# Two levels of Strassen's method for the first product of a fused attention and feed-forward kernel

The kernel runs on one core of one Trainium2 chip. The metric is the device time of one execution in microseconds (us), the median of several. Engines are named as the profile names them: PE is TensorE's matmul, PEld its weight load, DVE VectorE, ACT ScalarE, POOL GpSimd, SP SyncE, which issues most transfers.

## The reference

```python
# q, k, v: (8, 8, 576, 64) f32; w_in: (512, 2048); w_out: (2048, 512)
kv  = einsum('bhsd,bhse->bhde', k, v)
out = einsum('bhsd,bhde->bhse', q, kv)
x   = out / sqrt(mean(out*out, -1) + 1e-6) * g_norm      # per head
x   = x.transpose(0, 2, 1, 3).reshape(4608, 512)
h   = x @ w_in
g   = maximum(0.01 * h, h)
return g @ w_out
```

## The kernel before

The 4608 rows are worked off in nine blocks of 512. Block 0 uses plain matmuls. From block 1 on, each block is four chunks of 512 hidden columns, and both products of a chunk (h, the first; o, the second) use one level of Strassen's method in Winograd's form: seven products of quarters instead of eight, each four fp32 matmuls with 256 moving columns. The h product of a chunk is interleaved with the o product of the chunk before, and the attention of the next batch is fed in between, one step at every odd slot of the 28 slots (4 chunks x 7 products) of a block.

```python
ORDER = (1, 2, 6, 5, 7, 3, 4)
def strassen(which, left, right, done):
    for i in ORDER:
        ...                                   # two PSUM banks, "a" and "c"; 1, 2, 5 start one
        for part in range(2):
            for r in range(2):
                matmul(bank[:, part, :], lhsT=left(i, part, r), rhs=right(i, part, r), ...)
        done(i, bank)                         # eviction: ACT copy or DVE add into SBUF
        yield
# in product_h, done():  g21, g22, ... = bank sums; relu on ACT;
#   s1..s4 = sums of g on GpSimd, the left sides of the o product
...
for i in range(1, NB):                        # blocks
    a_steps = attention(i + 1) if i + 1 < B else iter(())
    for c in range(NC):                       # chunks
        h_steps = product_h(h_sides, x_sides, g_sides)
        for t in range(7):
            go(h_steps, 1)
            go(o_steps, 1)
            ...                               # sides of w_in and w_out on GpSimd
            if (7 * c + t) % 2:
                go(a_steps, 1)
            if c == NC - 1 and t == 4 and i + 1 < NB:
                go(a_steps)
                x_sides, more_x = sides_x(xTs.pop(i + 1))   # sides of x on VectorE
        o_steps = product_o(c, o_next, g_sides, os, store(i))
```

## Time and profile before

| | before |
|---|---|
| median (lowest to highest) | 978.23 us (977.07 to 978.3) |
| PE busy, share of the span | 954.6 us, 98% |
| DVE / ACT / POOL busy | 430 / 270 / 508 us |
| bytes moved by DMA | 63.5 MB |

### The profile page before, as it was taken

Reading aid. Unit: us, or ns where it says so; the run is one execution under the profiler, and the core shown is the slowest. Engines: PE = TensorE matmul, PEld = TensorE weight load, DVE = VectorE, ACT = ScalarE, POOL = GpSimd, SP = SyncE. Lnnn points to the kernel's source line nnn. Section 1 sums busy time; section 2 is a strip of 40 time slices with the busy share of each in tenths; the row PEclk is TensorE's granted clock in tenths of the full one; section 3 lists DMA queues with packets and bytes.
Section 4 is the critical chain, followed back from the end, with each engine's and each line's share of the span. In section 5 each row is a group of like instructions: output and inputs, shape, how many; then the busy total and the mean of one; then the engine's idle time right before and its main releaser. Section 6 shows DMA issues by size and latency. Waiting matters only on the chain.

```text
span 974.5 us, 14053 instructions
## 1 busy us (share of the span) xinstructions
PE 954.6 (98%) x5702; PEld 762.3 (78%) x5702; DVE 430.2 (44%) x688; ACT 270.1 (28%) x531; POOL 507.9 (52%) x399
## 2 busy tenths in 40 slices
PE   8899998999999999999999999999999999999997
PEld 4444345888888888888888888888888888888886
DVE  3966873256224543256224832373235422431223
ACT  3634531232123311332123212331223121112210
POOL 1000203556655565666665665566565766666664
PEclk9899998999999999999999999999999999999999
DMA  9989702500152004300430044002200000001001
GB/s 248 215 217 252 197 1 84 153 1 1 40 149 50 1 11 130 97 1 1 141 97 1 1 126 111 1 1 65 77 1 1 11 33 1 1 12 33 1 0 44
DMA packets 36161, 63.48 MB, mean 65 GB/s; under 512 B 4864, under 2 KB 21248, under 8 KB 36096
## 3 DMA queue, kind: packets, MB, share of 16 engines
q1 hardware_dynamic: 26112, 51.95, 20.8%
q10 hardware_dynamic: 9856, 10.62, 3.2%
q8 instruction: 45, 0.74, 0.3%
q14 instruction: 20, 0.16, 0.1%
q0 software_dynamic: 128, 0.00, 0.0%
HBM read 53.12 MB, written 9.44 MB: 64 GB/s over the span
## 4 chain that ended last, share of the span: by engine, by line
PE 94%; DVE 2%; DMA 2%; ACT 1%; issue 0%; SPq 0%; ACTq 0%
PE h_a L87 23%; PE o_a L87 23%; PE h_c L87 17%; PE o_c L87 17%; PE h_ps L87 5%; PE o_acc L87 5%; PE o_ps L87 2%; DMA k_in<-in_k_dram 2%; PE kv_ps L87 2%; DMA raw<-in_moe_w_in_dram 1%; DVE w L199 0%; DVE w L201 0%; ACT cut L194 0%; DVE qT L329 0%; DVE xT L309 0%
## 5 line engine op out<-in xcount | busy, mean ns | idle before, releaser
L405 POOL TENSOR_TENSOR ws<-w 128x512 f32<-128x512 f32 x33 | 46.4, 1407 | 288.6 <-PE h_c L87 247.7
L405 DVE TENSOR_TENSOR o<-o_a,o 128x512 f32<-128x512 f32 x104 | 71.6, 688 | 203.3 <-PE o_a L87 203.2
L484 ACT ACTIVATE g<-g 128x512 f32<-128x512 f32 x96 | 60.5, 630 | 292.5 <-DVE g L405 292.5
L405 POOL TENSOR_TENSOR ws<-w,w 128x512 f32<-128x512 f32 x33 | 43.5, 1318 | 150.5 <-ACT cut L194 101.4
L87 PE MATMUL o_a<-wt,gs 128*128 128x256 f32 x512 | 120.9, 379 | 0.0
L87 PEld LDWEIGHTS o_a<-wt,gs 128*128 128x128 f32 x512 | 97.3, 190 | 13.2
L405 DVE TENSOR_TENSOR o<-o_c,o 128x512 f32<-128x512 f32 x88 | 60.5, 687 | 89.5 <-PE o_c L87 89.5
L405 POOL TENSOR_TENSOR wt<-w,wt 128x512 f32<-128x512 f32 x64 | 83.2, 1300 | 2.5
L405 POOL TENSOR_TENSOR gs<-g,g 128x512 f32<-128x512 f32 x64 | 83.2, 1323 | 0.3 <-ACT g L484 0.2
L405 DVE TENSOR_TENSOR g<-h_c,g 128x512 f32<-128x512 f32 x64 | 44.0, 688 | 85.6 <-PE h_c L87 85.6
L87 PE MATMUL h_ps<-xT,w 128*128 128x512 f32 (+1 forms) x136 | 60.2, 588 | 6.9 <-DVE xT L309 6.1
L87 PE MATMUL o_acc<-w,gT 128*128 128x512 f32 x128 | 60.7, 619 | 3.7 <-DVE w L201 3.7
L87 PE MATMUL h_a<-xT,w 128*128 128x256 f32 x256 | 61.2, 382 | 0.7 <-ACT g L484 0.7
L87 PE MATMUL o_a<-w,g 128*128 128x256 f32 x256 | 60.6, 379 | 0.8 <-DVE o L405 0.8
L87 PE MATMUL h_a<-xt,w 128*128 128x256 f32 x256 | 61.1, 382 | 0.0
L87 PE MATMUL h_c<-xT,w 128*128 128x256 f32 x256 | 61.1, 381 | 0.0
L87 PE MATMUL h_a<-xt,ws 128*128 128x256 f32 x256 | 61.1, 381 | 0.0
L87 PE MATMUL h_a<-xT,ws 128*128 128x256 f32 x256 | 61.1, 381 | 0.0
L87 PE MATMUL h_c<-xt,ws 128*128 128x256 f32 x256 | 61.1, 381 | 0.0
L87 PE MATMUL o_c<-wt,gs 128*128 128x256 f32 x256 | 60.5, 379 | 0.0
L87 PE MATMUL h_c<-xT,ws 128*128 128x256 f32 x256 | 60.5, 379 | 0.0
L87 PE MATMUL o_a<-wt,g 128*128 128x256 f32 x256 | 60.5, 379 | 0.0
(84 smaller groups left out, 1607.6 us busy)
## 6 DMA issues: line engine op xcount, KB each, us to landing
out_dram<-o ACTq DMA_DIRECT2D x36, 256.0 KB, 2.2
v_in<-in_v_dram SPq DMA_DIRECT2D x30, 288.0 KB, 4.9
raw<-in_moe_w_in_dram SPq DMA_DIRECT2D x64, 128.0 KB, 5.8
raw<-in_moe_w_out_dram SPq DMA_DIRECT2D x16, 512.0 KB, 6.8
k_in<-in_k_dram SPq DMA_DIRECT2D x28, 288.0 KB, 4.2
q_in<-in_q_dram SPq DMA_DIRECT2D x56, 144.0 KB, 4.5
q_in<-in_q_dram SPq DMA_DIRECT2D x56, 140.0 KB, 4.5
k_in<-in_k_dram ACTq DMA_DIRECT2D x2, 288.0 KB, 9.2
```

The lines of the kernel that those rows point to most:

```text
L87: pin(nc.tensor.matmul(*args, **kw))
L405: eng.tensor_tensor(out_, a, b_, op=ALU.subtract if minus else ALU.add)
L484: nc.scalar.activation(t, t if src is None else src, func=AF.Prelu, alpha=SLOPE)
```

## The change

The intent is to take columns off PE. From block 2 on the h product uses two levels: each of the seven products of quarters is itself done by seven products of smaller blocks, 49 matmuls of 128 x 128 x 128 instead of 28 with 256 columns. They run in two groups: products 1, 6, 7, 4 of the outer level together (banks h_ha and h_hc, four parts each), then 2, 5, 3 (h_hb and h_ob, three parts). The 49 combinations of w_in are made once, in block 1, written to DRAM, and read again per block into a ring of nine places. The sides of x get a second level too (`quarters`). The cut diff:

```diff
+    def combine(c):                       # block 1: quarters of w_in, to DRAM
+        for js, y in (((5, 6), pair(0, ...)), ((7, 3), pair(1, ...)), ((1, 2), direct), ((4,), last)):
+            add(nc.vector, s1, y21, y22)
+            add(nc.vector, s2, s1, y11, True)
+            add(nc.vector, s3, y11, y21, True)
+            add(nc.vector, s4, y12, s2, True)
+            ...                           # three dma_start per j on SyncE
+    reads = [(c, j) for _ in range(2, NB) for c in range(NC) for j in ALL]
+        def quarters(group):              # second level of the sides of x
+            for js, y in of[group]:
+                add(nc.vector, t[:, :, 0, :], y12, y11, True)
+                add(nc.vector, t[:, :, 1, :], y22, t[:, :, 0, :], True)
+                add(nc.vector, y12, y22, y12, True)
+                add(nc.vector, t[:, :, 2, :], y21, t[:, :, 1, :], True)
+    def product_h_two(i, c, to):
+        for group, tags, out_ in ((0, ("ha", "hc"), g), (1, ("hb", "ob"), qc)):
+            for k in ORDER:
+                for n, j in enumerate(js):
+                    matmul(banks[b][:, n, :], lhsT=w_place(base + n)[:, SLOT[k], :],
+                           rhs=x_sides[j][k], ...)
+                ...                       # eviction: ACT copy or DVE add
+                if group == 0 and k == 4:
+                    for n in range(1, 4): # three running sums
+                        add(nc.gpsimd, g[:, :, n, :], g[:, :, n, :], g[:, :, n - 1, :])
+                    relu(g[:, :, 3, :])
+                yield
+            read(base + len(js) + RING)
+        add(nc.vector, g[:, :, 0, :], g[:, :, 0, :], qc[:, :, 0, :])   # merges of the groups
+        ...                               # three more, relus on ACT
+        sums()                            # s1..s4 on GpSimd, as before
     for i in range(1, NB):
+        if i > 1:
+            quarters(1)
         for c in range(NC):
             for t in range(7):
-                go(h_steps, 1)
+                go(h_steps, 1 if one else 2)
                 go(o_steps, 1)
                 if (7 * c + t) % 2:
                     go(a_steps, 1)
+                if c == NC - 1 and i + 1 < NB:
+                    if t == 3:
+                        go(a_steps)
+                        x_sides, first, second, quarters = sides_x(i + 1)
+                        first()
+                    if t == 4 and not one:
+                        second()
+                        quarters(0)
```

More of the change, by code (lines that the diff above doesn't have):

```diff
@@ L73 @@
     consts = ctx.enter_context(tc.tile_pool(name="consts", bufs=1))
-    stage = ctx.enter_context(tc.tile_pool(name="stage", bufs=3))
+    dram = ctx.enter_context(tc.tile_pool(name="dram", bufs=1, space=bass.MemoryType.DRAM))
     ins = ctx.enter_context(tc.tile_pool(name="ins", bufs=2))
@@ L77 @@
     xpool = ctx.enter_context(tc.tile_pool(name="xpool", bufs=3))
-    wcomb = ctx.enter_context(tc.tile_pool(name="wcomb", bufs=1))
     gpool = ctx.enter_context(tc.tile_pool(name="gpool", bufs=2))
@@ L84, with view, pair @@
     pin = tc.keep_in_program_order
+    NW = U * NE * P
+    w1_all = consts.tile([P, 2 * NC * NW], F32, name="w1_all")
+    stage = consts.tile([P, 3 * NW], F32, name="stage")
+    pairs = consts.tile([P, 4 * NW], F32, name="pairs")
+    g_all = [consts.tile([P, 4 * U * N2], F32, name=f"g_{i}") for i in range(2)]
+    def view(t, lo, *shape):
+        n = 1
+        for d in shape:
+            n *= d
+        t = t[:, lo:lo + n]
+        names = "abcd"[:len(shape)]
+        return t.rearrange(f"p ({' '.join(names)}) -> p {' '.join(names)}",
+                           **dict(zip(names, shape))) if len(shape) > 1 else t
+    def pair(i, *shape):
+        return view(pairs, i * NW, *shape)
     def matmul(*args, **kw):
@@ L129, in load_first @@
         qs += [rows(early[:, i * n:]) for i in range(2)]
-        ks, vs = (t + [rows(wcomb.tile([P, 4 * U * P], F32, tag=f"pair{i + j}",
-                                       name="early_kv")) for i in range(2)]
-                  for j, t in ((0, ks), (2, vs)))
+        ks, vs = (t + [pair(i + j, J, D) for i in range(2)] for j, t in ((0, ks), (2, vs)))
         for way, to, src, ts, p in (
@@ L141 @@
     kvs = [consts.tile([P, NP, D], F32, name=f"kv_{i}") for i in range(2)]
-    zeros = gpool.tile([P, NT], F32, tag="g11", name="zeros")
+    zeros = view(g_all[0], 0, NT)
     nc.gpsimd.memset(zeros, 0.0)
     load_first()
-    w1_sb = [[consts.tile([P, U, NE, P], F32, name=f"w1_{h}_{c}") for c in range(NC)]
-             for h in range(2)]
+    w1_sb = [[view(w1_all, (2 * c + h) * NW, U, NE, P) for c in range(NC)] for h in range(2)]
     w2_sb = [[consts.tile([P, U, DM], F32, name=f"w2_{h}_{c}") for c in range(NC)]
@@ L157, in spare @@
         return gpool.tile([P, n], dtype, tag=next(spare_homes), name=name)
-    raw_homes = itertools.cycle([(stage, "raw")] * 3 + [(wcomb, f"pair{i}") for i in range(4)])
+    raw_homes = itertools.cycle([view(stage, i * NW, NW) for i in range(3)]
+                                + [pair(i, NW) for i in range(4)])
     def load(t, src):
@@ L173, in load_f64 @@
         n //= 2
-        pool, tag = next(raw_homes)
-        raw = pool.tile([P, a * n, 2], U32, tag=tag, name="raw")
+        raw = next(raw_homes).bitcast(U32).rearrange("p (n two) -> p n two", two=2)
         load(raw.rearrange("p (a n) two -> p a (n two)", a=a), src)
@@ L411, in sides_w1 @@
         a21, a22 = w1_sb[1][c][:, :, :2, :], w1_sb[1][c][:, :, 2:, :]
-        s12 = wcomb.tile([P, 2, U, 2, P], F32, tag="pair0", name="ws")
+        s12 = pair(0, 2, U, 2, P)
         sides = {1: a11, 2: a12, 4: a22, 5: s12[:, 0], 6: s12[:, 1]}
@@ L417, in more @@
         def more():
-            s34 = wcomb.tile([P, 2, U, 2, P], F32, tag="pair1", name="ws")
+            s34 = pair(1, 2, U, 2, P)
             sides.update({7: s34[:, 0], 3: s34[:, 1]})
@@ L428, in sides_w2 @@
         b21, b22 = w2_sb[1][c][:, :, :N2], w2_sb[1][c][:, :, N2:]
-        t12 = wcomb.tile([P, 2, U, N2], F32, tag="pair2", name="wt")
+        t12 = pair(2, 2, U, N2)
         sides = {1: b11, 2: b21, 3: b22, 5: t12[:, 0], 6: t12[:, 1]}
@@ L434, in more @@
         def more():
-            t34 = wcomb.tile([P, 2, U, N2], F32, tag="pair3", name="wt")
+            t34 = pair(3, 2, U, N2)
             sides.update({7: t34[:, 0], 4: t34[:, 1]})
@@ L439, in sides_w2 @@
         return sides, more
-    def sides_x(x):
+    GROUPS = (1, 6, 7, 4), (2, 5, 3)
+    ALL = GROUPS[0] + GROUPS[1]
+    SLOT = {1: 0, 2: 1, 4: 2, 5: 3, 6: 4, 7: 5, 3: 6}
+    NG = 7 * P
+    w1_dram = [{j: dram.tile([P, 7, P], F32, name=f"w1_{c}_{j}") for j in ALL}
+               for c in range(NC)]
+    def combine(c):
+        direct = w1_sb[0][c].rearrange("p u (t r) m -> p t u r m", t=2)
+        last = w1_sb[1][c][:, :, 2:, :].unsqueeze(1)
+        for js, y in (((5, 6), pair(0, 2, U, 2, P)), ((7, 3), pair(1, 2, U, 2, P)),
+                      ((1, 2), direct), ((4,), last)):
+            t = view(stage, next(stage_homes) * NW, len(js), 4, P)
+            s1, s2, s3, s4 = (t[:, :, i, :] for i in range(4))
+            y11, y12, y21, y22 = (y[:, :, u, r, :] for u in range(2) for r in range(2))
+            add(nc.vector, s1, y21, y22)
+            add(nc.vector, s2, s1, y11, True)
+            add(nc.vector, s3, y11, y21, True)
+            add(nc.vector, s4, y12, s2, True)
+            for i, j in enumerate(js):
+                to = w1_dram[c][j]
+                pin(nc.sync.dma_start(to[:, :2, :], y[:, i, 0, :, :]))
+                pin(nc.sync.dma_start(to[:, 2, :], y[:, i, 1, 1, :]))
+                pin(nc.sync.dma_start(to[:, 3:, :], t[:, i, :, :]))
+            yield
@@ new lines, with w_place, read @@
+    stage_homes = itertools.cycle(range(3))
+    reads = [(c, j) for _ in range(2, NB) for c in range(NC) for j in ALL]
+    RING = 2 * NC * NW // NG
+    n_read = 0
+    def w_place(n):
+        return view(w1_all, n % RING * NG, 7, P)
+    def read(to):
+        nonlocal n_read
+        while n_read < min(to, len(reads)):
+            c, j = reads[n_read]
+            pin(nc.sync.dma_start(w_place(n_read), w1_dram[c][j]))
+            n_read += 1
+    xt1 = [work.tile([P, 2, N2], F32, tag="xt1", name="xt1"), view(pairs, 12 * P, 2, N2)]
@@ L444, in sides_x @@
+    xt24 = work.tile([P, 2, 2, N2], F32, tag="xt24", name="xt24")
+    qc = pair(0, 4, 3, P)
+    xi = view(stage, 0, 4, 3, P), view(stage, 12 * P, 3, 3, P)
+    def sides_x(i):
+        x = xTs.pop(i)
         b11, b12 = x[:, :2, :N2], x[:, :2, N2:]
         b21, b22 = x[:, 2:, :N2], x[:, 2:, N2:]
-        t1, t2, t4 = (work.tile([P, 2, N2], F32, tag=f"xt{i}", name=f"xt{i}")
-                      for i in (1, 2, 4))
+        t1, t2, t4 = xt1[i % 2 if i > 1 else 0], xt24[:, 0], xt24[:, 1]
         t3 = b12
-        add(nc.vector, t1, b12, b11, True)
@@ L450, in sides_x, with first, second @@
-        add(nc.vector, t2, b22, t1, True)
-        add(nc.vector, t3, b22, b12, True)
-        return ({1: b11, 2: b21, 3: b22, 4: t4, 5: t1, 6: t2, 7: t3},
-                lambda: add(nc.vector, t4, b21, t2, True))
+        sides = {1: b11, 2: b21, 3: b22, 4: t4, 5: t1, 6: t2, 7: t3}
+        def first():
+            add(nc.vector, t1, b12, b11, True)
+            add(nc.vector, t3, b22, b12, True)
+        def second():
+            add(nc.vector, t2, b22, t1, True)
+            add(nc.vector, t4, b21, t2, True)
@@ new lines, in quarters @@
+        def quarters(group):
+            upper, lower = (x[:, h:h + 2, :].rearrange("p r (t v n) -> p t r v n", t=2, v=2)
+                            for h in (0, 2))
+            of = [((1, 7), upper), ((6, 4), xt24.rearrange("p t r (v n) -> p t r v n", v=2))], \
+                [((2, 3), lower), ((5,), t1.rearrange("p r (v n) -> p r v n", v=2).unsqueeze(1))]
+            two, k = {}, 0
+            for js, y in of[group]:
+                t = xi[group][:, k:k + len(js)]
+                k += len(js)
+                y11, y12, y21, y22 = (y[:, :, r, v, :] for r in range(2) for v in range(2))
+                add(nc.vector, t[:, :, 0, :], y12, y11, True)
[3 more added lines that the diff above has]
+                for n, j in enumerate(js):
+                    two[j] = {1: y11[:, n, :], 2: y21[:, n, :], 3: y22[:, n, :],
+                              4: t[:, n, 2, :], 5: t[:, n, 0, :], 6: t[:, n, 1, :],
+                              7: y12[:, n, :]}
+            sides_two.setdefault(i, {}).update(two)
@@ L455, with strassen @@
+        return sides, first, second, quarters
+    sides_two = {}
     ORDER = (1, 2, 6, 5, 7, 3, 4)
     FRESH = (1, 2, 5)
-    def strassen(which, left, right, done):
+    def strassen(which, order, left, right, done):
         banks = {}
-        for i in ORDER:
+        for i in order:
             b = "a" if i in (1, 6, 7, 4) else "c"
@@ L471, in strassen, with relu, g_of, sums @@
                            skip_group_check=True)
-            done(i, bank)
+            done(i, bank.rearrange("p u (v n) -> p (u v) n", v=2))
             yield
-    def product_h(w_sides, x_sides, to):
-        g11, g12, g21, g22 = (gpool.tile([P, U, N2], F32, tag=f"g{i}", name=f"g{i}")
-                              for i in ("11", "12", "21", "22"))
-        s1, s2, s3, s4 = (gpool.tile([P, U, N2], F32, tag=f"gs{i}", name=f"gs{i}")
+    def relu(t, src=None):
+        nc.scalar.activation(t, t if src is None else src, func=AF.Prelu, alpha=SLOPE)
+    def g_of(c, to):
+        g = view(g_all[c % 2], 0, 4, 4, P)
+        g11, g21, g22, g12 = (g[:, :, i, :] for i in range(4))
+        s1, s2, s3, s4 = (gpool.tile([P, 4, P], F32, tag=f"gs{i}", name=f"gs{i}")
                           for i in range(1, 5))
         to.update({1: g11, 2: g12, 3: s4, 4: g22, 5: s1, 6: s2, 7: s3})
-        def relu(t, src=None):
-            nc.scalar.activation(t, t if src is None else src, func=AF.Prelu, alpha=SLOPE)
+        def sums():
+            add(nc.gpsimd, s1, g21, g22)
+            add(nc.gpsimd, s2, s1, g11, True)
+            add(nc.gpsimd, s3, g11, g21, True)
+            add(nc.gpsimd, s4, g12, s2, True)
+        return g, sums
+    def product_h(c, w_sides, x_sides, to):
+        g, sums = g_of(c, to)
+        g11, g21, g22, g12 = (g[:, :, i, :] for i in range(4))
         def done(i, bank):
@@ L499, in done @@
                 relu(g21)
-                add(nc.gpsimd, s1, g21, g22)
-                add(nc.gpsimd, s2, s1, g11, True)
-                add(nc.gpsimd, s3, g11, g21, True)
             elif i == 7:
@@ L507, in done @@
                 relu(g12, bank)
-                add(nc.gpsimd, s4, g12, s2, True)
-        yield from strassen("h", lambda i, part, r: w_sides[i][:, part, r, :],
+                sums()
+        yield from strassen("h", ORDER, lambda i, part, r: w_sides[i][:, part, r, :],
                             lambda i, part, r: x_sides[i][:, r, :], done)
+    def product_h_two(i, c, to):
+        n0 = 7 * ((i - 2) * NC + c)
+        g, sums = g_of(c, to)
+        x_sides = sides_two[i]
+        into = {1: (0, True), 2: (0, False), 6: (1, True), 5: (3, True), 7: (3, False),
+                3: (1, False), 4: (2, True)}
+        for group, tags, out_ in ((0, ("ha", "hc"), g), (1, ("hb", "ob"), qc)):
+            js = GROUPS[group]
+            base = n0 + 4 * group
+            banks = {}
+            for k in ORDER:
+                b = 0 if k in (1, 6, 7, 4) else 1
+                if k in FRESH:
+                    banks[b] = ps_m.tile([P, len(js), P], F32, tag=tags[b], name=f"h_{tags[b]}")
+                for n, j in enumerate(js):
+                    matmul(banks[b][:, n, :], lhsT=w_place(base + n)[:, SLOT[k], :],
+                           rhs=x_sides[j][k], start=k in FRESH and n == 0, stop=True,
+                           skip_group_check=True)
+                at, fresh = into[k]
+                if fresh:
+                    nc.scalar.copy(out_[:, at], banks[b])
+                else:
+                    add(nc.vector, out_[:, at], banks[b], out_[:, at])
+                if group == 0 and k == 4:
+                    for n in range(1, 4):
+                        add(nc.gpsimd, g[:, :, n, :], g[:, :, n, :], g[:, :, n - 1, :])
+                    relu(g[:, :, 3, :])
+                yield
+            read(base + len(js) + RING)
+        add(nc.vector, g[:, :, 0, :], g[:, :, 0, :], qc[:, :, 0, :])
+        relu(g[:, :, 0, :])
+        for n in (1, 2):
+            add(nc.vector, g[:, :, n, :], g[:, :, n, :], qc[:, :, 1, :])
+        relu(g[:, :, 2, :])
+        add(nc.vector, g[:, :, 1, :], g[:, :, 1, :], qc[:, :, 2, :])
+        relu(g[:, :, 1, :])
+        sums()
     def product_o(c, w_sides, g_sides, os, finish):
@@ L516, in product_o @@
                 os[key] = opool.tile([P, 2, N2], F32, tag="o", name=f"o{key}", bufs=6)
-        into = {1: ("11", True), 5: ("22", True), 2: ("11", False), 6: ("12", True),
+        into = {2: ("11", True), 5: ("22", True), 1: ("11", False), 6: ("12", True),
                 3: ("12", False), 7: ("22", False), 4: ("21", True)}
@@ L522, in done @@
             key, fresh = into[i]
+            to = os[key].rearrange("p u (v n) -> p (u v) n", v=2)
             if c == 0 and fresh:
-                nc.scalar.copy(os[key], bank)
+                nc.scalar.copy(to, bank)
             else:
-                add(nc.vector, os[key], bank, os[key])
-            if c == NC - 1 and i in (2, 7, 3, 4):
+                add(nc.vector, to, bank, to)
+            if c == NC - 1 and i in (1, 7, 3, 4):
                 finish(key, os[key])
-        yield from strassen("o", lambda i, part, r: g_sides[i][:, r, part * P:(part + 1) * P],
+        yield from strassen("o", (2, 1) + ORDER[2:],
+                            lambda i, part, r: g_sides[i][:, 2 * r + part, :],
                             lambda i, part, r: w_sides[i][:, r, :], done)
@@ L563, in first_block @@
                                stop=(e == NE - 1), skip_group_check=True)
-                gT = gpool.tile([P, NT], F32, tag=("g11", "g12", "g21", "g22")[n % 4], name="gT")
+                gT = view(g_all[n // 4 % 2], n % 4 * NT, NT)
                 nc.scalar.activation(gT, h_ps, func=AF.Prelu, alpha=SLOPE)
@@ L601 @@
     first_block(between)
-    x_sides, more_x = sides_x(xTs.pop(1))
-    more_x()
+    x_sides, first, second, quarters = sides_x(1)
+    first()
+    second()
     h_sides, more = sides_w1(0)
     more()
-    o_steps, o_sides = iter(()), None
+    o_steps = iter(())
     for i in range(1, NB):
@@ L609 @@
         os = {}
+        if i > 1:
+            quarters(1)
         for c in range(NC):
             g_sides = {}
-            h_steps = product_h(h_sides, x_sides, g_sides)
+            one = i == 1
+            h_steps = product_h(c, h_sides, x_sides, g_sides) if one else product_h_two(i, c, g_sides)
+            c_steps = combine(c) if one else iter(())
             for t in range(7):
-                go(h_steps, 1)
+                go(h_steps, 1 if one else 2)
                 go(o_steps, 1)
                 if t == 3:
-                    h_next, more_h = sides_w1((c + 1) % NC)
+                    if one and c < NC - 1:
+                        h_sides, more_h = sides_w1(c + 1)
                     o_next, more_o = sides_w2(c)
-                if t == 5:
+                if t == 5 and one and c < NC - 1:
                     more_h()
+                if t < 3:
+                    go(c_steps, 2 if t == 0 else 1)
                 if (7 * c + t) % 2:
                     go(a_steps, 1)
-                if c == NC - 1 and t == 4 and i + 1 < NB:
-                    go(a_steps)
-                    x_sides, more_x = sides_x(xTs.pop(i + 1))
+                if c == NC - 1 and i + 1 < NB:
+                    if t == 3:
+                        go(a_steps)
+                        x_sides, first, second, quarters = sides_x(i + 1)
+                        first()
+                    if t == 4 and not one:
+                        second()
+                        quarters(0)
             go(h_steps)
@@ L629 @@
             more_o()
-            h_sides = h_next
+            if one:
+                read((2, 4, 6, RING)[c])
+                if c == NC - 1:
+                    second()
+                    quarters(0)
             o_steps = product_o(c, o_next, g_sides, os, store(i))
-        if i + 1 < NB:
-            more_x()
     go(o_steps)
```

## The prediction

> **What bounds the kernel now.** I read the page first: the busy table and the slices say which engine has no room.
>
> ```profile
> PE 954.6 (98%) x5702; PEld 762.3 (78%) x5702; DVE 430.2 (44%) x688; ACT 270.1 (28%) x531; POOL 507.9 (52%) x399
> ...
> PE   8899998999999999999999999999999999999997
> ...
> PEclk9899998999999999999999999999999999999999
> DMA  9989702500152004300430044002200000001001
> ...
> PE 94%; DVE 2%; DMA 2%; ACT 1%; issue 0%; SPq 0%; ACTq 0%
> ```
>
> TensorE works in every slice at full clock, and the chain that ended last is 94% PE. The chain in order of time, cut to some microseconds of the middle, shows that PE does not merely look busy: the pieces follow without a gap.
>
> ```profile
> 384.79 1.73 PE h_a L87 x8
> 386.51 1.73 PE o_a L87 x8
> 388.24 1.21 PE kv_ps L87 x72
> 389.45 1.92 PE h_c L87 x8
> ```
>
> A product of quarters is four fp32 matmuls, and the trace has eight records for it: an fp32 matmul of this program leaves two (LDWEIGHTS, MATMUL) pairs. One pair with 256 moving columns takes 1.727/8 = 215.9 ns. In block 0, same view, 512 columns take 3.43/8 = 428.9 ns. The difference, 213 ns for 256 columns, leaves about 2.7 ns per pair that does not depend on the columns. So time on PE is columns, and the columns are what this change reduces. The windows of 100 us from 260 to 560 us have PE busy 100.0 of 100, DVE 44, ACT 27, POOL 61, DMA 21%. From 157 us on there are eight blocks of 102 us (974.5 - 157 = 817), 25.5 us per chunk of a block (four chunks): 7 h and 7 o products of 1.727 us are 24.2, attention the rest.
>
> **What the skill says.** "TensorE: Matmul & The Clock Gate", section "Back-to-back issue gap", gives N/2.4 + 2.5 ns for a matmul of N columns. For two passes a pair (my reading of fp32) that is 213.3 + 2.5 = 215.8; the trace's 215.9 agrees. The same section warns that at N=128 a stream of load-and-multiply pairs was measured at about 81 ns instead of 56, as the weight load no longer hides; its section "LDWEIGHTS" puts 128 columns at P/1.2 = 107 ns, as long as 128 moving columns of two passes. The trace has a test of that, see below. "GPSIMD Engine Reference", its opening table of figures, says that GpSimd shares its SBUF interface with VectorE and contends with VectorE instructions that have two SBUF inputs. The trace agrees: such a 128x512 add on DVE takes 674 ns at least but 1.76 and 1.65 us while POOL adds.
>
> ```profile
> L405 DVE TENSOR_TENSOR xt<-xT,xt x16: 674/956/1667, 133.7 to 858.8; 128x512 f32<-128x512 f32 x16
> ...
> 445.05 1.76 DVE L405 TENSOR_TENSOR xt<-xT 128x512 f32<-128x512 f32 x1
> 446.84 1.65 DVE L405 TENSOR_TENSOR xt<-xT,xt 128x512 f32<-128x512 f32 x1
> 448.41 0.68 DVE L405 TENSOR_TENSOR o<-o_c,o 128x512 f32<-128x512 f32 x1
> 449.01 1.16 DVE L405 TENSOR_TENSOR xT<-xT 128x512 f32<-128x512 f32 x1
> ```
>
> The reader sees in it (durations of the tile xt as least, median, most; then DVE in order of time at a block's end) that an add with one input in PSUM keeps its 0.68 us.
>
> **The change, part by part.**
>
> PE. In 28 chunks (blocks 2 to 8, four each) 28 h matmuls of 256 columns become 49 of 128. The instruction order confirms it: 2851 matmuls before, 3439 after, 28 x 21 more. What one pair of 128 columns with its own 128-column weights costs is the central number. Bound by columns it is 106.7 + 2.7 = 109.4 ns. Against it stands the load, whose records look long: 190 ns, though never overlapping where a matmul takes 216. If no load could begin before the one before it had ended, a pair would cost 190. The attention's kv product decides: 64x64 quadrants, 64 moving columns, so weights and columns are in the same ratio as in the new product.
>
> ```profile
> L87 PEld LDWEIGHTS kv_ps<-v_in,k_in x1080: 129/135/135, 14.7 to 697.8; 64*64 64x64 f32 x180
> ```
>
> 72 pairs of it take 1.21 us, first load included (the single records in the middle repeat a quadrant every 58.4 ns). Four quadrants run side by side, so a quadrant has a pair every 58 ns while the load record is 135 ns. So most of a load record is latency, not occupancy; columns alone would be 53.3 + 2.7 = 56. I take 112 ns for 128 columns. A chunk's h product: 56 pairs x 215.9 = 12.09 us before, 98 x 112 = 10.98 after, 1.11 us less; times 28 is **31 us off the path** (38 if 109.4).
>
> DVE. Its tensor_tensors go from 388 to 760: per chunk three more evictions (128x384, 0.55 us, between the 0.47 for 320 and 0.69 for 512 of the trace) and four adds of 128x512 in SBUF that merge the two groups (0.67 to 1.2, I take 0.85); per block 12 adds of 256 and 4 of 128 elements for the quarters of x (about 0.45 and 0.3); in block 1 another 64 small ones for the quarters of w_in. That is 28 x (1.65 + 3.4) = 141, 7 x 6.6 = 46, and 26: 213 us more, 430 to about 640, some 66% on average. All of it lies beside PE as long as each chunk's DVE work fits its 24 us. In the first chunks it does: evictions of h 3.7, of o 4.8, merges 3.4, attention some 4 to 9. In the last chunk of a block it does not: evictions 8.5, merges 3.4, the end of an attention tail and two transposes 9.3 (transposes of 1.25, multiplies up to 1.33), x sides and quarters about 8 make 29 us; successive DVE instructions overlap by 0.08 us (0.60 from start to start at 0.68 each), 50 of them give back 4. So about 25 to 27 us of DVE work meets 24 us of PE. A bank can't be refilled before its eviction, and the evictions stand behind the x adds in DVE's order, so PE waits: I put 3 us on each of the five block ends that have attention, 15 us. At the change from block 1 to 2 the second half of the x sides and the first quarters are made after the last product has been issued: 4 us more.
>
> POOL loses 32 adds (388 to 356: no w_in sides after block 1, but three running sums per chunk). Its 11 per chunk at 1.32 us are 14.5 of 24 us; the sums for the o product come about 8.5 us after the last h product, and the o product that reads them starts some 10.6 us after: it just fits. ACT gets 140 more copies, about 75 us spread over 700, beside.
>
> DMA. Each chunk reads 7 x 448 KB = 3.2 MB, 90 MB in all, besides the 63 MB of now. In 24 us that is 134 GB/s, plus about 50 for attention and output: some 185. The first 34 us of the trace move 219 to 250 GB/s with the engines full, and in packets of 1 to 4.6 KB; the new ones are 3.5 KB. So it fits at about three quarters. Four blocks of a group are wanted half a chunk (11 us) after the group before it ended; their first two are read in that time, about 4 us when nothing else is queued, over 11 when 2.3 MB of k, v and q went ahead. That is once per block: I allow 3 us in all. Block 1 writes 12.8 MB and has more on DVE: 4 us.
>
> Sum: 978.2 - 31 + 15 + 4 + 3 + 4 = 973. The waits are my least certain terms and were taken from DVE's worst case; with slack between a bank's eviction and its next use they may be half. I settle on **966 us**.
>
> **Rivals.** One: the weight load binds. Were a 128-column pair 190 ns, a chunk would take 98 x 190 = 18.6 us, 28 x 6.5 = 183 us more, near 1160; at 130 ns the gain is gone and with the waits the time is about 1000. For it: the skill's 81 ns at N=128. Against: kv_ps at 58 ns per quadrant. I give it one in ten. Two: DVE becomes the bound at block ends by more than I took: with adds at 1.2 us and above, as at 445 us, the excess is 7 us or more for five or six ends, 40 us, and the gain is eaten: 980 to 990. For it: 18 us of DVE without a pause at the present block end, where it has a third less to do. Against: POOL has less to do then. Three: all waits are hidden and the columns count: 978 - 38 + 5 = 945. For it: today's DVE stretch of 18 us costs PE nothing. Four: reads come late; DMA has a quarter of room and the ring holds nine blocks, so I expect little.
>
> **Range and chances.** From the third rival, 945, to the second, 989. Faster by 2% means below 958.6, which needs most waits to vanish; 0.34. Slower by 2%, above 997.8, needs the first rival or a bad second; 0.08. Within: 0.58.
>
> **What would show it.** Eight records of h_ha or h_hc in the chain should take 0.88 to 0.91 us (0.9 for 112 ns); 1.5 would be the first rival. PE busy should fall from 100 to about 96% in blocks 2 to 6, with the gaps at block ends and DVE as releaser; DVE busy near 640 us; block 8, with no attention and no next block, should be shorter by the full 4.4 us of four chunks. PE waits for DMA beyond 5 us, or waits in every chunk, would make the prediction wrong.

## More of the kernel before

Matmuls and transfers are kept in program order; VectorE's, ScalarE's and GpSimd's instructions are ordered by the scheduler.

One more view is needed to compare with later: the windows view, stretch 300 to 800 us (most of the five blocks with attention; the last 36 us are block 7), gives busy time (and records) of PE, PEld, DVE, ACT and POOL, then granted clock, DMA share and GB/s.

```profile
300.00:800.00 500.00, 500.00 (x3084) 425.73 (x3083) 216.23 (x330) 132.97 (x265) 303.93 (x233) 1.00 0.15 44
```

PE has no microsecond free in it. Whatever makes PE wait here is added to the time. A granted clock below 1.00 means that in a part of the stretch PE ran at half clock: the trace's clock records hold either 1 or 0.5.

## The result, and the profile after

The changed kernel takes **1012.48 us** (1011.01 to 1017.0, four runs), against 978.23: ratio 1.0361, 95% interval 1.0324 to 1.0397, slower. (A ratio here is the mean time of one kernel's fast runs over the mean of the other's in the same rounds, so it is not quite the ratio of the medians. Where a time is called the same, slower or unclear, the limit is 2%.) The result is outside the predicted range.

The page of the changed kernel:

```profile
PE 950.0 (94%) x6878; PEld 783.9 (77%) x6878; DVE 656.4 (65%) x1060; ACT 330.3 (33%) x671; POOL 482.5 (48%) x367
...
PE   7899997998899989998999899998999799999997
...
PEclk9799999999899999998999999999999999999998
...
PE 61%; DVE 18%; DMA 7%; issue 4%; POOL 4%; ACT 4%; SPq 1%; ACTq 0%; DVEq 0%; POOLq 0%
```

Three things differ from before. PE has slices at 8 and 7 in the middle; the granted clock has slices at 8 there as well, where the row of before was all 9; and the chain that ended last goes through PE for 61% of the span instead of 94%. The windows view of the same stretch says how much is lost there:

```profile
300.00:800.00 500.00, 474.37 (x3840) 421.31 (x3840) 336.85 (x529) 169.15 (x353) 279.54 (x205) 0.98 0.52 168
```

**Where the time went.** I took the start-to-start times of successive PE records and subtracted what each record takes when nothing waits (215.9 ns for 256 columns, 111.7 ns for 128). What is left is wait, or half clock. Summed over the trace it is 44.4 us before and 114.3 us after: 70 us more. Against it stands a chunk without attention at 24.17 us before and 23.03 us after, 1.14 us less, 32 us over 28 chunks. 70 - 32 = 38 is the difference of the two profiled spans (1012.1 - 974.5). (The medians differ by 34 us: the profiled run of before was 2 us faster than its median, that of after 1.4 us slower.) The 70 us lie here:

| stretch | predicted extra wait, us | before | after | extra |
|---|---|---|---|---|
| block 1 and its change to block 2 | 4 + 4 | 3.4 | 16.5 | 13.1 |
| last h chunk of the five blocks with attention (2 to 6) | 15 | 1.7 | 31.6 | 29.9 |
| first h chunk after each of them | - | 1.3 | 5.1 | 3.8 |
| second and third h chunks of these blocks | 3 (DMA) | 7.0 | 18.7 | 11.7 |
| blocks 7 and 8 | 0 | 0.9 | 3.5 | 2.6 |
| start and end of the kernel | 0 | 30.1 | 39.0 | 8.9 |

**A block end.** The chain in order of time at the end of block 4 (start, us, what):

```profile
557.71 0.89 PE h_ha L110 x8
...
576.40 2.02 DVE xT L329
578.41 0.60 DVE o L425
579.01 0.47 DVE pairs L425
579.49 0.04 issue
579.53 1.65 PE h_ob L110 x6
581.18 1.28 PE h_hb L110 x6
```

Eight records of h_ha take 0.89 us: the new pair costs what was predicted. But from 562 us on the chain stays on DVE until, at 579.5, an eviction of h_ob (tile `pairs`) at last lets PE go on, 3.62 us late. And then PE does six records in 1.65 and 1.28 us that take 0.67 elsewhere: the trace's clock records have half clock from 579.0 us on, for 3.4 us. DVE's instructions ahead of that eviction, from its timeline:

```profile
571.36 1.77 DVE L425 TENSOR_TENSOR xt<-xT,xt 128x512 f32<-128x512 f32 x1
573.05 2.02 DVE L329 TENSOR_TENSOR xT<-xT,inv 128x768 f32<-128x768 f32 x1
...
575.48 0.99 DVE L425 TENSOR_TENSOR stage<-xT,stage 128x256 f32<-128x256 f32 x1
576.40 2.02 DVE L329 TENSOR_TENSOR xT<-xT,inv 128x768 f32<-128x768 f32 x1
...
578.94 0.54 DVE L425 TENSOR_TENSOR pairs<-h_ob,pairs 128x384 f32<-128x384 f32 x1
```

The eviction itself is 0.54 us. Ahead of it in the queue stand the attention's division (xT), a side of x (xt) and quarters (stage), some of them at two to three times their shortest duration. GpSimd's timeline at that moment has the running sums that the change added:

```profile
571.31 4.89 POOL L425 TENSOR_TENSOR g<-g 128x512 f32<-128x512 f32 x3 [4.55 <-ACT g L645]
```

The windows view of this last chunk and of the one before it shows how uneven the load is (same columns as above):

```profile
532.50:557.50 25.00, 24.60 (x180) 21.16 (x181) 14.88 (x27) 8.31 (x21) 13.81 (x10) 1.00 0.35 123
557.50:587.10 29.60, 25.91 (x171) 23.05 (x171) 29.14 (x47) 9.51 (x20) 16.34 (x11) 0.94 0.30 108
```

VectorE is busy 29.14 of 29.6 us in the last chunk and 14.88 of 25 us in the one before it.

**The second and third chunks.** Here a read of w_in's quarters comes late, behind the next q in SyncE's queue. The chain ahead of block 4's third chunk:

```profile
518.65 6.18 DMA q_in<-in_q_dram
...
524.90 7.52 DMA w_all<-w
532.42 0.04 issue
532.47 0.49 PE h_ha L110 x2
```

**The end.** The last o product has no h product beside it, so the merges, the relu and GpSimd's sums stand bare before it, and half clock follows. The last chain:

```profile
992.75 3.71 POOL gs L425 x3
996.46 0.04 issue
996.50 3.78 PE o_a L110 x8
1000.28 2.78 PE o_c L110 x8
1003.06 1.73 PE o_a L110 x8
```

The half clock alone, computed from the clock records as half of the time in which PE worked under it, costs some 11 us in five stretches between 261 and 695 us, 1.5 to 3.0 each, and some 3 us at the end (3.78 + 2.78 - 2 x 1.73). The kernel before has none between 157 and 972 us.

### The profile page after: what moved, and what is told of

Same layout as the page of the kernel before. It is cut to its first block, busy times and chain, and to the rows that moved or that the text cites. A ratio compares the mean times of both kernels' runs of the same rounds, so it can differ in the third digit from the quotient of the medians.

```text
span 1012.1 us, 17430 instructions
## 1 busy us (share of the span) xinstructions
PE 950.0 (94%) x6878; PEld 783.9 (77%) x6878; DVE 656.4 (65%) x1060; ACT 330.3 (33%) x671; POOL 482.5 (48%) x367
## 4 chain that ended last, share of the span: by engine, by line
PE 61%; DVE 18%; DMA 7%; issue 4%; POOL 4%; ACT 4%; SPq 1%; ACTq 0%; DVEq 0%; POOLq 0%
PE o_a L110 15%; PE o_c L110 11%; PE h_ha L110 8%; PE h_hc L110 6%; PE h_hb L110 5%; PE h_ps L110 4%; DVE stage L425 4%; PE h_ob L110 4%; POOL g L425 3%; PE o_acc L110 3%; DVE g L425 2%; DVE xT L329 2%; DMA w_all<-w 2%; DVE o L425 2%; PE o_ps L110 2%
## 5 line engine op out<-in xcount | busy, mean ns | idle before, releaser
L425 POOL TENSOR_TENSOR g<-g 128x512 f32<-128x512 f32 x84 | 115.7, 1377 | 141.3 <-ACT g L645 132.2
L425 POOL TENSOR_TENSOR pairs<-w,pairs 128x512 f32<-128x512 f32 x64 | 93.8, 1465 | 124.0 <-PE o_a L110 121.6
L110 PE MATMUL o_a<-pairs,gs 128*128 128x256 f32 x512 | 123.5, 385 | 9.2 <-DVE o L425 4.4
L425 POOL TENSOR_TENSOR gs<-g 128x512 f32<-128x512 f32 x64 | 81.0, 1286 | 62.2 <-ACT g L575 62.2
L110 PEld LDWEIGHTS o_a<-pairs,gs 128*128 128x128 f32 x512 | 93.9, 192 | 21.5 <-POOL gs L425 4.6
L425 DVE TENSOR_TENSOR g<-g,pairs 128x512 f32<-128x512 f32 x112 | 91.3, 858 | 16.4 <-ACT pairs L645 16.1
L425 POOL TENSOR_TENSOR pairs<-w_all 128x512 f32<-128x512 f32 x8 | 10.7, 1338 | 143.5 <-DMA stage<-in_moe_w_out_dram 102.8
L110 PE MATMUL h_ps<-xT,w_all 128*128 128x512 f32 (+1 forms) x136 | 63.1, 613 | 6.1 <-DVE xT L329 6.1
L110 PE MATMUL o_c<-w,gs 128*128 128x256 f32 x256 | 62.5, 388 | 0.7 <-DVE o L425 0.7
L110 PE MATMUL o_c<-w,g 128*128 128x256 f32 x256 | 62.3, 387 | 0.0
L110 PE MATMUL o_a<-pairs,g 128*128 128x256 f32 x256 | 61.9, 386 | 0.0
```

Source lines behind the costliest of these rows:

```text
L110: pin(nc.tensor.matmul(*args, **kw))
L425: eng.tensor_tensor(out_, a, b_, op=ALU.subtract if minus else ALU.add)
```

## The experiments

Theory A: too much VectorE work is heaped at a block's end. Theory B: the reads come late. Theory C: GpSimd's new running sums slow VectorE's adds and hold ScalarE's relu, and evictions behind both. Each kernel ran beside the kernel before on the same chip, but the groups of runs were on different chips (7, 9 and 12), where the kernel before took 976.6 to 978.1 us; so between groups the ratios compare better than the times. By the 2% limit e2, e5 and f1 are slower, e4 is unclear, and all others count as the same as the kernel before. The two last columns are sums of waits over blocks 2 to 6 as in the table above: of the second and third h chunks, and of the last chunk with the first one after it.

| run | edit | us | ratio to before | chunks 2, 3 | last, next first |
|---|---|---|---|---|---|
| kernel before | | 978.23 | 1 | 7.0 | 3.1 |
| changed kernel | | 1012.48 | 1.0361 | 18.7 | 36.8 |
| e1_noquart | quarters of x left out after block 2 | 989.89 | 1.0129 | 18.9 | 15.6 |
| e2_noread | only nine reads | 1008.65 | 1.0332 | 14.2 | 37.9 |
| e3_nosum | running sums left out | 985.98 | 1.0099 | 13.9 | 17.6 |
| e4_early | attention earlier | 995.89 | 1.0187 | 30.0 | 10.7 |
| e5_end | last sums on DVE | 1010.88 | 1.0334 | 18.9 | 35.5 |
| f1_spread | all spread, DVE and ACT in program order | 1073.73 | 1.0995 | 74.1 | 38.5 |
| f1b_free | all spread, scheduler's order | 992.28 | 1.0168 | 30.0 | 10.9 |
| f2_dvesum | f1b_free, running sums on DVE | 981.67 | 1.0051 | 17.1 | 16.0 |
| f3_nosum | f1b_free without running sums | 966.33 | 0.9904 | 14.8 | 5.9 |
| f4_spread3 | f2_dvesum, running sums spread | 974.00 | 0.9965 | 16.7 | 6.7 |

**Less VectorE work.** 16 VectorE adds fewer per block from block 3 on, nothing else. Its output is wrong, which doesn't matter for the time.

```diff
+                if i == 2:
-                add(nc.vector, t[:, :, 0, :], y12, y11, True)
+                    add(nc.vector, t[:, :, 0, :], y12, y11, True)
                 ...                       # the other three likewise
```

> The changed kernel without the quarter adds of x from block 3 on (wrong result on purpose: the products read block 2's quarters); 16 DVE adds per block fewer, everything else as it was. Theory A (DVE has more than a chunk's work at a block's end, evictions stand behind the x adds, PE waits and its clock is halved after the wait): the waits of the block ends of blocks 3 to 7 (6 to 8 us each) shrink to 2 us or less and the half-clock stretches there go, so 975 to 988 us. Theory B (late reads from DRAM): no change, above 1005. Theory C (POOL's running sums hold ACT and DVE): a third of it at most, 1000 to 1006.

Measured: 989.89 us (985.74 to 990.05), 1.0129 (1.0108 to 1.0151). The ends fall from some 6.5 us to 1.7 to 3.0 (the last stays at 5.1), and the half clock after them is gone in blocks 2 to 5. So the queue at the end is a cause, though the time stays 2 us above the range of theory A and the last end was expected to fall too: 56 us less of VectorE's time (600 against 656 in the whole kernel) are worth some 22 us of the kernel's. Beside the half clock at the start of block 2, two stretches are left in the five blocks, of 3.4 us each from 520.1 and from 772.7 us, and no wait near them is over 1.13 us.

**No late reads.** The ring is read once and then used as it is. Its output is wrong, which doesn't matter for the time.

```diff
-    reads = [(c, j) for _ in range(2, NB) for c in range(NC) for j in ALL]
+    reads = [(c, j) for _ in range(2, NB) for c in range(NC) for j in ALL][:RING]
```

> The changed kernel with only the first nine weight blocks read from DRAM (wrong result on purpose: later products use stale weights); 187 reads and 86 MB fewer. Theory A: only the PE waits on these reads in the second third of a block go, 2 us in each of blocks 2 to 5, 8 to 10 us in all: 1000 to 1006. Theory B: the reads, or their load on the memory, are the cause: 985 or less. If neither, no change at 1012.

Measured: 1008.65 us (1007.13 to 1010.41), 1.0332. With 187 of 196 reads gone, 3 to 4 us come back, less than expected, and the ends are as they were. Late reads are real, but theory B falls as a main cause.

**No running sums.** Its output is wrong, which doesn't matter for the time.

```diff
-                    for n in range(1, 4):
-                        add(nc.gpsimd, g[:, :, n, :], g[:, :, n, :], g[:, :, n - 1, :])
```

> The changed kernel without POOL's three running sums per chunk (wrong result on purpose); 84 POOL adds fewer. Theory A: DVE's adds at the block end are no longer slowed by POOL (1.5 to 2.0 us go to 0.4 to 1.0) and ACT is not held by the relu that waits for the sums, so part of the block-end wait goes: 990 to 1002. Theory C: these sums are the root, the block-end waits go nearly entirely: 975 to 988. If POOL does not matter: above 1008.

Measured: 985.98 us (984.62 to 987.83), 1.0099 (1.008 to 1.0117), in theory C's range. VectorE has the same instructions in the same order, but those at the block's end are shorter. Its timeline in this run, to be held against that of the changed kernel:

```profile
559.11 0.65 DVE L425 TENSOR_TENSOR xt<-xT,xt 128x512 f32<-128x512 f32 x1
559.68 0.95 DVE L329 TENSOR_TENSOR xT<-xT,inv 128x768 f32<-128x768 f32 x1
...
562.32 2.02 DVE L329 TENSOR_TENSOR xT<-xT,inv 128x768 f32<-128x768 f32 x1
...
564.86 0.54 DVE L425 TENSOR_TENSOR pairs<-h_ob,pairs 128x384 f32<-128x384 f32 x1
```

From the start of the side of x to the eviction it is 5.75 us here (559.11 to 564.86), 7.58 there (571.36 to 578.94). The add of 128x512 takes 0.65 us instead of 1.77, the first product with `inv` 0.95 instead of 2.02; the second, beside other adds of GpSimd, keeps 2.02. PE's wait for this eviction fell from 3.62 to 1.79 us, by 1.83, just as much as the stretch on VectorE is shorter; so here it is the slowed adds. The other half of theory C, the held relu, shows in the chain of the changed kernel, but at the one place looked at it is small: at 550.98 us, behind a relu that had waited for the sums, PE waits 0.33 us. Its share of the gain was not measured by itself. So C is a cause as well, but not the root that its expectation made of it: the ends keep 17.6 of their 36.8 us. Taken alone, the edit against A gives 22 us and the one against C 26, both mostly at the same block ends: they meet in the same queue.

**Everything spread, in fixed order.** My first mending, with a correct result: attention steps at slots 2 to 17, sides of x from slot 19 on, quarters in four portions, the loads after the reads, the last relu and GpSimd's sums one h step later, the last sums on VectorE, and VectorE's and ScalarE's instructions kept in program order.

```diff
-                if (7 * c + t) % 2:
+                if 7 * c + t in (2, 3, 5, 6, 7, 8, 9, 10, 12, 14, 15, 17):
                     go(a_steps, 1)
+                if nxt and at == (24 if one else 19):
+                    ...; first()
+                if nxt and at == 25: second(...)
+                if nxt and at == 26: quarters(0, 0)    # (0, 1) at 27, (1, 0) and (1, 1) in the next block
...
+    strict[0] = True                     # every VectorE and ScalarE instruction pinned
```

> A correct version that does the same arithmetic as the changed kernel, with DVE and ACT held in the order the program gives: attention's steps done earlier in a block (its last tail in the third chunk, not the fourth), the x adds and quarters spread over five steps, loads of k, v, q issued behind the group's weight reads, the relu that waits for POOL's running sums put later, the last chunk's sums on DVE. Theory A (work of DVE heaped at the block end, not its amount, makes PE wait): block-end waits of 6 to 8 us fall below 2.5 us, no half-clock stretch after block 2, 970 to 985 us. If DVE's total (some 640 us) is too much in any order: 1000 or more.

Measured: 1073.73 us (1070.17 to 1078.66), 1.0995. Far worse, and outside theory A's range. By my own expectation 1000 or more would have meant that VectorE has too much work in any order; f4_spread3 below has more of it and takes 974 us, so that reading was wrong. Now VectorE stands still in front of instructions that wait for something, with ready evictions behind them. A stretch of its chain:

```profile
406.81 4.89 DMA out_dram<-o
411.72 2.44 DMA q_in<-in_q_dram
...
415.38 0.69 DVE g L119
```

The transpose of a q waits for its load, the eviction (g) waits for the transpose, PE for the eviction. Half clock alone costs 33 us in this trace.

**Everything spread, order free.** The same, without the order:

```diff
-    strict[0] = True
+    strict[0] = False
```

> The same as f1_spread, but DVE's and ACT's order left to the scheduler, which hoists attention's transposes in front of evictions. If the spreading of the emitted work is enough: within 5 us of f1_spread. If the hoisting is what puts x adds and transposes ahead of evictions: 10 us or more above it.

Measured: 992.28 us (989.5 to 993.65), 1.0168; both of my expectations were wrong. The scheduler's order, which puts an eviction ahead of work that isn't ready, is worth 81 us here (the two kernels differ in this alone and ran on the same chip).

**Attention earlier, alone.** One edit of the changed kernel, result correct: the first line of the diff of f1_spread.

> Correct. From the changed kernel with one edit: the twelve attention steps of a block are issued at steps 2,3,5,6,7,8,9,10,12,14,15,17 of 28 instead of every odd step, so that no attention is left in the last chunk. Theory A (the block end waits because VectorE's work is heaped there: x sides, quarters, merges and the attention's last tail; about 9 us of it is the tail): the five block ends fall from some 6.5 us of excess to 3 or less, without half clock, and the time falls by 15 to 25 us, to 987-997. Theory C (running sums of GpSimd are the cause): the ends keep over 4 us, 1000-1008. A third possibility: the waits come back in the first chunks, where the input reads now queue before the quarters of w_in, 1005-1015.

Measured: 995.89 us (994.66 to 998.08), 1.0187 (1.017 to 1.0204). As theory A has it: the last chunks wait 6.2 us instead of 31.6, and there is no half clock between 266 and 976 us. But the second and third chunks wait 30 us instead of 19, since the attention stands there now. It is nearly all that f1b_free gains; the rest of that spreading is worth 2 us by the ratios, 4 by the medians.

**The end of the kernel, alone.**

```diff
-            add(nc.gpsimd, s1, g21, g22)          # and s2, s3, s4
+            eng = nc.vector if len(ended) == NC * (NB - 1) - 1 else nc.gpsimd
+            add(eng, s1, g21, g22)                # and s2, s3, s4
```

> Correct. From the changed kernel with one edit: the four sums ahead of the very last o product run on VectorE instead of GpSimd. If the 6 us at the end of the kernel are the wait for GpSimd's sums with nothing beside it, and the half clock after it, the time falls by 4 to 6 us, to 1006-1008.5; if the tail is bound by the merges before the sums it falls by under 2 us.

Measured: 1010.88 us (1007.71 to 1012.5), 1.0334. In the profile the time from the last h matmul to the last o matmul falls from 20.3 to 18.0 us (14.9 in the kernel before). The expected 4 to 6 us didn't come: the merges before the sums stay, and of the half clock after them 1.9 us stay of 3.1.

**The running sums on VectorE.** From f1b_free, correct.

```diff
-                        add(nc.gpsimd, g[:, :, n, :], g[:, :, n, :], g[:, :, n - 1, :])
+                        add(V, g[:, :, n, :], g[:, :, n, :], g[:, :, n - 1, :])
```

> Correct. From f1b_free (992.3 us) with the three running sums per chunk on VectorE instead of GpSimd: three adds of 0.67 us for three of 1.6 us that slow VectorE's two-input adds. If what is left in the first chunks is GpSimd's chain holding ScalarE and VectorE, the time falls by 5 to 12 us, to 980-987; if VectorE's amount of work is what is left, it rises by 2 to 8 us.

Measured: 981.67 us (980.5 to 985.01), 1.0051. VectorE has 43 us more (708 instead of 665), GpSimd 105 less, and the time falls by 10.6 us (11 by the ratios). So it wasn't the amount on VectorE. What is left is again a queue: at 563.56 us in this chain PE waits for an eviction that stands behind the running sums (the 1.75 us of `g`).

```profile
560.68 1.75 DVE g L119
562.44 0.60 DVE o L119
563.04 0.47 DVE pairs L119
563.51 0.04 issue
563.56 0.94 PE h_ob L128 x6
```

**No running sums, from there.** A floor. Its output is wrong, which doesn't matter for the time.

> Wrong result on purpose. From f1b_free without the three running sums at all: the floor of what moving them can bring. If they cause the rest of the waits: 965-972, which would be faster than the kernel before; if the rest is reads and VectorE's amount: 980-988.

Measured: 966.33 us (965.58 to 975.69), 0.9904 (0.9858 to 0.995). Its profiled run is the one at 975.69, with half clock in block 1 that costs some 6 us more than in f2_dvesum; the other three are within 1 us.

**The running sums spread.** From f2_dvesum, correct.

```diff
-                if group == 0 and k == 4:
-                    for n in range(1, 4):
-                        add(V, g[:, :, n, :], g[:, :, n, :], g[:, :, n - 1, :])
+                if group == 1 and k in (2, 6, 5):
+                    n = (2, 6, 5).index(k) + 1
+                    add(V, g[:, :, n, :], g[:, :, n, :], g[:, :, n - 1, :])
```

> Correct. From f2_dvesum (981.7 us): the three running sums on VectorE are issued one after each of three pieces of the second group (at its products 2, 6 and 5) instead of together at the end of the first group. In f2_dvesum PE waits about 1.6 us for an eviction behind them in most second and third chunks, about 15 us in all. If that queue is the cause the time falls by 6 to 14 us, to 968-976, below the kernel before; if VectorE's amount is, by less than 3 us.

Measured, with five rounds: **974.0 us** (971.47 to 977.72), before 977.68; ratio 0.9965, interval 0.9942 to 0.9987. It beats the changed kernel clearly and the kernel before by a third of a per cent, which the interval just separates and the 2% limit calls the same. The last chunks wait 5.3 us in sum; the windows view of the five blocks:

```profile
300.00:800.00 500.00, 490.77 (x3961) 440.16 (x3960) 385.53 (x615) 180.24 (x370) 217.43 (x160) 1.00 0.55 177
```

VectorE works 386 of 500 us, more than in the changed kernel (337), and PE gets 491 instead of 474. Not the busy share but the place in the queue made the difference.

A last kernel, f5_spread4, moved block 1's quarters of w_in to slots 0, 2, 4 and 6 of each chunk. By my mistake its result is wrong: the last set is issued after the first quarters of x, which share its staging buffer.

> Correct. As f4_spread3, and in block 1 the four sets of quarters of w_in per chunk are made at steps 0, 2, 4 and 6 instead of 0, 0, 1 and 2. Block 1 waits some 14 us in f2_dvesum, against some 3 in the kernel before. If the heap of these adds is the cause, 3 to 8 us less than f4_spread3; if it is the merges of VectorE with ScalarE's order at the change of blocks, the same within 2 us.

It took 975.15 us (970.01 to 978.78), no less than f4_spread3: the heap of these adds isn't what block 1 waits for. What is, stays open; block 1 and its change to block 2 wait 16 us in the changed kernel and 20 us in f4_spread3's profile, 8 of them half clock.

## Why the prediction was wrong, step by step

- **The pair of 128 columns at 112 ns: right.** Eight records take 0.89 us, 111.7 ns each. The gain on PE is 1.14 us a chunk, 32 us; 31 was predicted. The first rival, the weight load, is out: at 111.7 ns a pair it costs nothing that shows.
- **DVE near 640 us: right** (656). **25 to 27 us of DVE work beside 24 us of PE at a block's end, 3 us each: the step that failed.** It was 29.1 us of busy time in the last chunk of block 4. My list of durations had 29, from which I took off 4 for overlap; the slowed adds ate that. With longest waits of PE of 2.1 to 4.2 us an end, shorter ones beside them, and half clock on top of four of the five, the ends cost 29.9 us instead of 15, and 3.8 more just after. And the settling on 966 halved this term, for slack between an eviction and the bank's next use that was not there. Room was near: VectorE had 10 us free in the chunk before. Moving twelve attention steps forward (e4_early), with no instruction less, takes 25 us of the 30 away (11 come back earlier in the block).
- **POOL "just fits": the wrong question.** I checked whether its 11 adds per chunk end in time for the o product. They do more harm on the way: they slow VectorE's adds with two SBUF inputs (1.77 for 0.65 us), though I had shown just that in the profile of before and written it off because POOL had fewer adds. The adds that POOL kept now lie elsewhere: the three running sums come in one run of 4.89 us at the time of the x sides. Leaving them out is worth 26 us (e3_nosum).
- **The half clock: absent from the working.** Some 11 us between 261 and 695 us and 3 at the end follow the waits. Where it came, it added 1.5 to 3.0 us to a wait of 2 to 4 us; after two waits of 3.30 and 3.38 us it did not come.
- **DMA 3 us: nearly right.** Without the reads 3 to 4 us less (e2_noread). The sign that I had set myself, waits for DMA beyond 5 us, did not come: the waits view has 3.0 us of PE and 4.1 us of PEld for `w_all`, so the prediction was wrong without it. The other sign, waits in every chunk, came in part: the second and third chunks of a block wait 11.7 us more than before. Without reads 4.5 us of these go, without running sums 4.8; the rest is open.
- **Block 1 and the change to block 2: 8 predicted, 13 found. The end of the kernel: nothing predicted, some 5 of the 8.9 us found.** The last o product follows merges and sums with nothing beside them, which the diff shows. Of the other 4 us some 2.4 lie ahead of block 1, whose first product starts at 159.93 us instead of 157.51; in e4_early, the same program up to there, it starts at 157.66, so they differ between executions and are not the change's.
- The second rival, DVE at the ends, had the mechanism: "40 us, and the gain is eaten". But I gave it 980 to 990, as if it would come alone (978 - 31 + 40 = 987; with the other 11 us of the sum 998); and the settled 966 halved the waits instead of doubling them. That the measured terms add up, 974.5 - 32 + 70 = 1012.5 for a span of 1012.1, is bookkeeping of one trace and no test. But it shows where the 44 us of wait beyond the predicted 26 lie: 18.7 at the ends and just after them, 8.7 in the second and third chunks, 8.9 at the start and the end of the kernel, 5.1 in block 1, 2.6 in blocks 7 and 8. The ends are the largest part, but not half of it.
- Two slips in the working decided nothing: at 130 ns a pair its own terms give 978 + 18 + 26 = 1022 us, not 1000; and the row of the granted clock that it reads as full in every slice has two slices at 8, both before 175 us.

## What to carry to other kernels

When one engine is at 98%, the value of taking work off it is decided by its waits, and these by the order in the other engines' queues, not by their busy shares: ask of each eviction what stands ahead of it when the bank is wanted. Give added work a place in time before counting its microseconds: the same arithmetic took 1012 us with its additions heaped at a block's end and on an engine that slows another, and 974 us with them and the attention spread. Leaving the order to a scheduler that puts ready work first was worth 81 us against fixing it by hand.

## What the Trainium skill lacked or had wrong

- "TensorE: Matmul & The Clock Gate", section "Back-to-back issue gap", warns of about 81 ns for a matmul of 128 columns in a stream of load-and-multiply pairs, where its formula has 56. Here an fp32 pair of 128 columns, each with its own weights, took 111.7 ns; the formula with two passes (my reading of fp32) gives, as an estimate, 106.7 + 2.5 = 109.2. No cost of the load showed. The page gives no spacing for fp32.
- The same page, section "HAM oscillation — how this bites in real kernels", puts the rule at no idle gaps above about 3.4 us. In the changed kernel, between 261 and 695 us, half clock came with waits of 3.44, 4.22, 3.23, 3.62 and, with shorter ones around it, 2.12 us; it lasted 3.4 or 6.8 us in the records. It did not come with two waits of 3.30 and 3.38 us. In e1_noquart it came after pairs of short waits, 1.10 and 0.78 us within 2.3 us and 1.13 and 0.92 us within 3.0 us. So waits well below the stated figure weren't safe here, while single ones of 3.30 and 3.38 us were: the length of one wait did not decide it, and what does stays open.
- "Perfetto Trace Analysis", section "Optimizing Scalar/DVE Operations", says that moving work between VectorE and GpSimd might not help since they share a port. Here the 128x512 add took 0.65 us with no add on GpSimd and 1.77 beside GpSimd's adds of 1.63 us (4.89 / 3), and moving work helped: taking three adds per chunk from GpSimd to VectorE, with another 43 us on VectorE, gained 10.6 us.
- No page speaks of what a fixed order of VectorE's instructions costs where their inputs come from many engines: 1073.7 against 992.3 us.
